# Two-input decode attention on one core: B's x loaded in 8-byte chunks behind the first K tile

## The chip, the cores and the metric

The kernel runs on one core of one Trainium2 chip. The metric is device microseconds (us) from start to end. An execution under the profiler has its own time, and a span (first to last instruction) that is a little shorter.

A core has a matrix engine (PE), a vector engine (DVE), an activation engine (ACT), a general engine (POOL) and a sync engine (SP). They run their own instruction streams and meet at semaphores. SP issues nearly all transfers here. A transfer is cut into packets that go to up to 16 DMA engines; each engine works through its own list in order. In this text such a list is called a ring: 16 rings, one per DMA engine. Behind the packets of a transfer each ring that took part writes the transfer's semaphore.

## The reference

Two independent attention blocks, A and B, each decode one token; their outputs are concatenated. Both have 32 heads of width 128, 8192 cached positions, and a model width of 512, all in bf16:

```
q      = (x @ wq)                  # x 1 x 512, wq 512 x 4096: 32 heads x 128
scores = q . K^T / sqrt(128)       # K per block 32 x 8192 x 128: 64 MB
p      = softmax(scores)
o      = p . V                     # V per block 32 x 8192 x 128: 64 MB
y      = o @ wo                    # wo 4096 x 512: 4 MB
out    = concat(y_A, y_B)          # 1 x 1 x 1024
```

Each K and V element is used once, so nearly all traffic is K and V: 4 x 64 MB, beside 4 MB for each of the four weight matrices and 1 KB for each x.

## The kernel before, in words

**Steps.** The work goes in 16 steps n = 0..15: 8 of A (n = 0..7), then 8 of B. A step takes four heads. Its K is one tile of 8 MB, 128 partitions x 256 positions x 128, 32 partitions to a head. `kn` holds two such tiles (slots n % 2), `vn` one V tile of the same size. In a step DVE multiplies the K tile by q in four chunks of 128 x 8192 (line 342, `plan_mul`). PE adds up the products by 16 matmuls with an identity per chunk (line 351, `plan_red`), and DVE reduces the result to scores (line 362, `plan_sr`). Then come the maximum (lines 368 to 391), the exponentials on ACT (line 399), and one step later the 256 matmuls with V (line 420, `plan_pv`). The last step is followed by the output projection (lines 478 and 505) and the output transfers.

**Loads.** All loads are issued by SP through `dma` (line 246) in the order in which the plan puts them. K of step n + 2 waits until step n has been summed (`red_done`), V of step n until the matmuls with the V before are done (`pv_done`), V of step 0 until all of q is made (`q_done[1]`). At the start SP issues five transfers without a wait: wq of A (4 MB, into the first half of `vn`), x of A, x of B (1 KB each), K of step 0 (8 MB), wq of B (4 MB, into the second half of `vn`). K of step 1 comes next. It goes to slot 1 of `kn`, and since the two x lie in partition 0 of that slot (`xrow`, with `KX = 1`), it waits for `x_ready`.

**x and q.** x arrives as one row in one partition. For each block four matmuls with a row of ones (line 302) spread it over the partitions, and ACT copies the result into `xb` (line 306). Before the change both blocks do this at the start, A through the PSUM tile `misc`, B through `qyp`; `x_ready` is the copy for B, the later one. `plan_q(a, j)` then makes q of four steps at a time: 16 matmuls with wq (line 320) into `qyp`, and an ACT copy into `qbc` (line 328). `qbc` has 16 slots of 128 elements per partition, 8 for A and 8 for B (`QA = 8`). q of A is made at the start. q of B is made inside step 0: on PE behind the third `plan_red`, ahead of the fourth.

**Order.** The order on each engine is written out by hand. PE runs steps 1 to 15 and the matmuls with V in a loop, and a final part comes after it. Names that the steps below touch: `load_k`, `load_x`, `load_wq`, `load_v`, `plan_x`, `plan_q`, `plan_red`, `plan_pv`, and the semaphores `s_x`, `s_w`, `s_k`, `s_v`.

Of the kernel before, what the change touches and what calls it, by code (L numbers as in the profile page):

```python
# [11 lines left out]
P = 128  # L12
# [11 lines left out]
class _Plan:  # L24
# [15 lines left out]
    def op(self, eng, fn, ctr=None, needs=(), inc=1):  # L40

        for m in needs:
            self.wait(eng, m)
        self.prog[eng].append((fn, ctr, inc))
        if ctr is None:
            return None
        ctr.n += inc
        return ctr, ctr.n
# [81 lines left out]
def bass_concat_heads__mha_block_cached__gqa_block_cached__decode_kernel(  # L130
# [13 lines left out]
    xs = [A_x, B_x]  # L144
# [4 lines left out]
    NA = 2  # L149
    H, Sk, Dh = ks[0].shape[1:]  # L150
    D = xs[0].shape[2]
    NOUT = wos[0].shape[1]
    assert Dh == P and H == 32 and D == 512 and NOUT == 512
    C = D // P
# [6 lines left out]
    QA = H // G  # L161
    NM = NA * QA
    NK = 2
    CT = 64
    NCH = T // CT
# [9 lines left out]
    with ExitStack() as st:  # L175
        ec = st.enter_context

        def sb(name, shape, dt):
            return ec(nc.sbuf_tensor(name, shape, dt))

        kn = sb("kn", [P, NK, T, Dh], BF16)
        vn = sb("vn", [P, T, Dh], BF16)

        def flat(ap):
            return ap.rearrange("p t d -> p (t d)")
# [5 lines left out]
        KX, KW = 1, (NM - 2) % NK  # L191
        wo_sb = [flat(kn[:, KW])[:, a * W:(a + 1) * W].rearrange("p (j n) -> p j n", n=NOUT)
                 for a in range(NA)]
        xrow = flat(kn[0:1, KX])[:, 0:NA * D].rearrange("p (a d) -> p a d", a=NA)
        xb = sb("xb", [P, NA, C, P], BF16)
        qbc = sb("qbc", [P, NM, Dh], BF16)
        pt = sb("pt", [P, T, G], BF16)
        s_sb = sb("s_sb", [P, T], F32)
        ones_bf = sb("ones_bf", [P, P], BF16)
# [19 lines left out]
        def ps(name, shape):  # L219
            return ec(nc.psum_tensor(name, shape, F32))  # L220
# [5 lines left out]
        misc = ps("misc", [P, 512])  # L226
        qyp = ps("qyp", [P, 512])
# [3 lines left out]
        op, wait = pl.op, pl.wait  # L231

        def ctr(name):
            return _Ctr(nc, st, name)

        s_x = ctr("s_x")
        s_w = [ctr("s_w%d" % a) for a in range(NA)]
        s_wo = [[ctr("s_wo%d%d" % (a, i)) for i in range(len(WOG[a]))] for a in range(NA)]
        s_k = [ctr("s_k%d" % i) for i in range(NK)]
# [2 lines left out]
        c_pool, c_dve, c_act, c_pe = ctr("c_pool"), ctr("c_dve"), ctr("c_act"), ctr("c_pe")  # L242
        c_mul, c_red, c_sr, c_pv = ctr("c_mul"), ctr("c_red"), ctr("c_sr"), ctr("c_pv")

        def dma(eng, dst, src, c, needs=()):
            return op(eng, lambda e: e.dma_start(dst, src), c, needs, inc=16)


        def const(fn, needs=()):
            return op("POOL", fn, c_pool, needs)  # L250

        i_onesb = const(lambda e: e.memset(ones_bf[:], 1.0))
# [15 lines left out]
        k_in, v_in, wq_in, wo_in = {}, {}, {}, {}  # L268
        red_done, pv_done, q_done, wo_done = {}, {}, {}, {}

        def quad(c, n):
            a, i = divmod(n, QA)
            return c[a][0, G * i:G * (i + 1)].rearrange("h (p t) d -> (h p) (t d)", p=HP)

        def load_k(n):
            k_in[n] = dma("SP", flat(kn[:, n % NK]), quad(ks, n), s_k[n % NK],
                          [x_ready if n == KX else red_done.get((n - NK, NCH - 1))])

        def load_v(n, cuts=(0, T)):
            dst, src = flat(vn[:]), quad(vs, n)  # L280
# [4 lines left out]
        def load_wq(a):  # L285
            wq_in[a] = dma("SP", wq_buf[a], wqs[a].rearrange("(p c) n -> p (c n)", p=P), s_w[a])

        def load_wo(a, g):
            h0, n = WOG[a][g]
            src = wos[a][h0 * Dh:(h0 + n) * Dh, :].rearrange("(p j) n -> p (j n)", p=P)  # L290
            wo_in[a, g] = dma("SP", wo_sb[a][:, h0:h0 + n, :].rearrange("p j n -> p (j n)"), src,
                              s_wo[a][g], [red_done[NM - 2, NCH - 1]])


        load_wq(0)
        x_in = [dma("SP", xrow[0:1, a, :], xs[a][0], s_x) for a in range(NA)][-1]

        for a in range(NA):
            def xmm(e, a=a):
                r = None  # L300
                for c in range(C):
                    r = e.matmul((misc if a == 0 else qyp)[:, c * P:(c + 1) * P],  # L302
                                 xrow[0:1, a, c:D:C], ones_bf[0:1, :], start=True, stop=True)
                return r
            m = op("PE", xmm, c_pe, [x_in, i_onesb])
            x_ready = op("ACT", lambda e, a=a: e.copy(
                xb[:, a].rearrange("p c m -> p (c m)"), (misc if a == 0 else qyp)[:]), c_act, [m])
        misc_free, qy_free = [x_ready], [x_ready]

        qbc_ready = {}  # L310

        def plan_q(a, j):

            def mm(e):
                r = None
                for hh in range(G):
                    for c in range(C):
                        w = wq_sb[a][:, c, 4 * G * j * Dh:4 * G * (j + 1) * Dh].rearrange(
                            "p (i h d) -> p i h d", h=G, d=Dh)[:, :, hh, :]
                        r = e.matmul(  # L320
                            qyp[hh * HP:(hh + 1) * HP, :].rearrange("p (i d) -> p i d", d=Dh),
                            xb[:, a, c, hh * HP:(hh + 1) * HP], w,
                            start=(c == 0), stop=(c == C - 1))
                return r
            m = op("PE", mm, c_pe, [x_ready, wq_in[a], qy_free[0]])
            q_done[a] = m
            n0 = a * QA + 4 * j
            qy_free[0] = op("ACT", lambda e: e.copy(  # L328
                qbc[:, n0:n0 + 4, :].rearrange("p i d -> p (i d)"), qyp[:]), c_act, [m])
            for n in range(n0, n0 + 4):  # L330
                qbc_ready[n] = qy_free[0]
# [8 lines left out]
        def plan_mul(n, c):  # L340
            k = kn[:, n % NK, c * CT:(c + 1) * CT, :]
            mul_done[n, c] = op("DVE", lambda e: e.tensor_tensor(  # L342
                k, k, qbc[:, nth(n), :].broadcast_to([P, CT, Dh]), ALU.mult),
                c_mul, [k_in[n], qbc_ready[n]])

        def plan_red(n, c):

            def mm(e, i0):
                r = None
                for i in range(Dh // DW):  # L350
                    r = e.matmul(  # L351
                        rps[:, c % 2, :].rearrange("p (t d) -> p t d", d=DW), ident[:],
                        kn[:, i0, c * CT:(c + 1) * CT, i * DW:(i + 1) * DW],
                        start=(i == 0), stop=(i == Dh // DW - 1))
                return r
            by_slot = (n % NK, [lambda e, i=i: mm(e, i) for i in range(NK)])
            red_done[n, c] = op("PE", by_slot, c_red, [
                i_ident, mul_done[n, c],
                sr_done[n, c - 2] if c > 1 else sr_done.get((n - 1, c + NCH - 2))])

        def plan_sr(n, c):
            sr_done[n, c] = op("DVE", lambda e: e.tensor_reduce(  # L362
                s_sb[:, c * CT:(c + 1) * CT],
                rps[:, c % 2, :].rearrange("p (t d) -> p t d", d=DW), AX.X, ALU.add),
                c_sr, [red_done[n, c], p_done.get(n - 1)])
# [62 lines left out]
        def plan_o(n):  # L428
            o_done[n] = op("DVE", lambda e: e.tensor_tensor(  # L429
                oD[:].rearrange("p a h -> p (a h)")[:, nth(n, G)], acc[:, 0:G],  # L430
                rinv[:, nth(n), :].rearrange("p o g -> p (o g)"), ALU.mult),
                c_dve, [pv_done[n], r_done[n]])
# [93 lines left out]
        cuts = {n: [] for n in range(L0, L1 + 1)}  # L526
        dcuts = []

        load_k(0)
        load_wq(1)  # L530
        ahead = len(pl.prog["SP"])
        plan_sel()
# [2 lines left out]
        for n in range(NM):  # L535
            if n >= L0:
                cuts[n].append(len(pl.prog["PE"]))
                dcuts.append(len(pl.prog["DVE"]))
            if n + 1 < NM:
                load_k(n + 1)  # L540
            else:
                load_wo(0, 0)
                for g in range(BEFORE):
                    load_wo(1, g)
            plan_mul(n, 0)
            plan_red(n, 0)
            plan_mul(n, 1)
            plan_red(n, 1)
            plan_sr(n, 0)
            plan_mul(n, 2)  # L550
            plan_red(n, 2)
            plan_sr(n, 1)
            plan_mul(n, 3)
            plan_sr(n, 2)
            if n == 0:
                for j in range(QA // 4):
                    plan_q(1, j)
            else:
                cuts[n].append(len(pl.prog["PE"]))
                plan_sum(n - 1)  # L560
                for t0, t1 in zip(VLAST, VLAST[1:]):
                    plan_pv(n - 1, t0, t1)
                cuts[n].append(len(pl.prog["PE"]))
                plan_o(n - 1)
            plan_red(n, 3)
            plan_sr(n, 3)
            plan_max(n)
            plan_gmax(n)
            plan_exp(n)
            load_v(n, VLAST if n == NM - 1 else (0, T))  # L570
# [112 lines left out]
```

## Time and profile before

| what | value |
|---|---|
| median of 3 runs | 667.17 us (666.86 to 667.19) |
| the profiled execution | 666.95 us |
| its span | 665.7 us |
| mean granted PE clock | 0.773 |
| busy share of the span: PE, DVE, ACT | 66%, 51%, 9% |
| moved | 285.33 MB, mean 429 GB/s |
| transfer packets | 6076, of them 690 under 512 bytes |

The profile's page cuts the span into 40 equal slices; a digit is the busy share of a slice in tenths. The windows view gives the same for chosen stretches. A row of the timeline is: start in us, duration in us, engine, line, operation, output tile <- input tile, sizes, count, and in brackets how long the engine had been idle before and what ended that. `SPq` rows are SP's issues of transfers; their duration is the time to issue, not to land. A row of waits is: engine, line, what was waited for, total us, times, longest us. A row of transfer issues ends with the median time from issue to landing. Line numbers are those of the kernel before.

### The profile page before, as it was taken

Reading aid. Unit: us, or ns where it says so; the run is one execution under the profiler, and the core shown is the slowest. Engines: PE = TensorE matmul, PEld = TensorE weight load, DVE = VectorE, ACT = ScalarE, POOL = GpSimd, SP = SyncE. Lnnn points to the kernel's source line nnn. Section 1 sums busy time; section 2 is a strip of 40 time slices with the busy share of each in tenths; the row PEclk is TensorE's granted clock in tenths of the full one; section 3 lists DMA queues with packets and bytes.
Section 4 is the critical chain, followed back from the end, with each engine's and each line's share of the span. In section 5 each row is a group of like instructions: output and inputs, shape, how many; then the busy total and the mean of one; then the engine's idle time right before and its main releaser. Section 6 shows DMA issues by size and latency. Waiting matters only on the chain. (4 is left out here: it accounts for less than half of the span.)

```text
span 665.7 us, 12460 instructions
## 1 busy us (share of the span) xinstructions
PE 440.0 (66%) x5649; PEld 253.2 (38%) x5649; DVE 340.4 (51%) x216; ACT 62.4 (9%) x151; POOL 3.0 (0%) x16
## 2 busy tenths in 40 slices
PE   1165776938388593838759483875948387694875
PEld 0022342616135261613526161442626144262655
DVE  1085908466390736638183563808356381835510
ACT  1002002020200102020110202010020201002020
POOL 1000000000000000000000000000000000000000
PEclk9999857768786676878767687966768787776875
DMA  9999999999999999999999999999999999999997
GB/s 378 435 447 438 438 432 417 425 437 441 425 437 441 441 425 422 433 441 433 429 441 437 437 421 425 441 437 425 441 437 441 421 425 437 441 425 437 414 439 303
DMA packets 6076, 285.33 MB, mean 429 GB/s; under 512 B 690, under 2 KB 948, under 8 KB 1204
## 3 DMA queue, kind: packets, MB, share of 16 engines
q1 hardware_dynamic: 6056, 285.22, 99.3%
q8 instruction: 6, 0.10, 0.1%
q14 instruction: 2, 0.02, 0.0%
q10 hardware_dynamic: 12, 0.00, 0.0%
HBM read 285.21 MB, written 0.00 MB: 428 GB/s over the span
## 5 line engine op out<-in xcount | busy, mean ns | idle before, releaser
L351 PE MATMUL rps<-kn,ident 128*128 128x512 bf16 x1024 | 291.2, 452 | 168.2 <-DVE kn L342 168.2
L342 DVE TENSOR_TENSOR kn<-kn,qbc 128x8192 bf16<-128x8192 bf16 x64 | 281.5, 4419 | 97.3 <-DMA kn<-in_A_k_cache_dram 57.6
L351 PEld LDWEIGHTS rps<-kn,ident 128*128 128x128 bf16 x1024 | 111.7, 113 | 334.8 <-issue 258.8
L420 PE MATMUL acc<-pt,vn 128*128 128x4 bf16 x4096 | 109.3, 165 | 9.8 <-DMA vn<-in_B_v_cache_dram 4.4
L420 PEld LDWEIGHTS acc<-pt,vn 128*128 128x128 bf16 x4096 | 108.6, 100 | 10.6 <-DMA vn<-in_B_v_cache_dram 4.8
L362 DVE TENSOR_REDUCE s_sb<-rps 128x64 f32<-128x512 f32 x64 | 44.0, 688 | 108.6 <-PE rps L351 108.6
L399 ACT ACTIVATE pt<-s_sb,negb 32x256 bf16<-32x256 f32 x64 | 54.9, 857 | 1.9
L391 ACT ACTIVATE negb<-bmp 128x1 f32<-128x1 f32 x16 | 2.7, 171 | 527.1 <-PE bmp L387 527.1
L429 DVE TENSOR_TENSOR oD<-acc,rinv 128x4 f32 (+1 forms) x16 | 2.6, 162 | 96.1 <-PE acc L420 84.9
L387 PE MATMUL bmp<-gm,hrow 1*128 1x1 f32 x128 | 17.6, 254 | 6.0 <-DVE gm L377 6.0
L387 PEld LDWEIGHTS bmp<-gm,hrow 1*128 1x128 f32 x128 | 16.2, 195 | 10.7 <-DVE gm L377 10.0
L374 PE MATMUL mtp<-ident_f,m 128*1 128x128 f32 x32 | 6.1, 270 | 19.8 <-DVE m L368 19.8
L399 ACT ACTIVATION_READ_ACCUMULATOR pt<-s_sb,negb 32x1 f32 x64 | 15.9, 248 | 0.0
L374 PEld LDWEIGHTS mtp<-ident_f,m 128*1 128x1 f32 x32 | 1.4, 80 | 27.7 <-DVE m L368 27.7
L302 PE MATMUL misc<-ones_bf,kn 1*128 1x128 bf16 x4 | 0.6, 302 | 13.1 <-DMA kn<-in_B_x_dram 13.1
L377 DVE TENSOR_REDUCE gm<-mtp 1x4 f32<-1x128 f32 x16 | 4.5, 279 | 7.5 <-PE mtp L374 7.5
L404 PEld LDWEIGHTS misc<-rsum,ones_f 128*128 128x128 f32 x32 | 6.2, 197 | 3.6 <-issue 1.4
L320 PE MATMUL qyp<-vn,xb 128*32 128x512 bf16 x64 | 6.0, 504 | 2.2 <-ACT qbc L328 1.5
L368 DVE TENSOR_REDUCE m<-s_sb 128x1 f32<-128x256 f32 x16 | 6.7, 420 | 0.5
L478 PE MATMUL qyp<-o,kn 128*128 128x1 bf16 x192 | 5.5, 165 | 1.7 <-issue 1.4
L478 PEld LDWEIGHTS qyp<-o,kn 128*128 128x128 bf16 x192 | 5.4, 103 | 1.9 <-issue 1.5
L328 ACT CAST qbc<-qyp 128x512 bf16<-128x512 f32 x4 | 2.3, 586 | 38.7 <-PE qyp L320 38.7
(39 smaller groups left out, 30.9 us busy)
## 6 DMA issues: line engine op xcount, KB each, us to landing
vn<-in_B_v_cache_dram SPq DMA_DIRECT2D x1, 6144.0 KB, 22.6
vn<-in_A_wq_dram SPq DMA_DIRECT2D x1, 4096.0 KB, 12.4
vn<-in_B_wq_dram SPq DMA_DIRECT2D x1, 4096.0 KB, 39.9
kn<-in_A_wo_dram SPq DMA_DIRECT2D x1, 4096.0 KB, 36.0
kn<-in_B_wo_dram SPq DMA_DIRECT2D x1, 2048.0 KB, 40.5
vn<-in_B_v_cache_dram SPq DMA_DIRECT2D x1, 2048.0 KB, 27.0
kn<-in_B_wo_dram SPq DMA_DIRECT2D x1, 1024.0 KB, 29.0
kn<-in_B_wo_dram SPq DMA_DIRECT2D x1, 512.0 KB, 29.8
```

The costliest lines, as they stand in the source:

```text
L320: r = e.matmul(qyp[hh * HP:(hh + 1) * HP, :].rearrange("p (i d) -> p i d", d=Dh), xb[:, a, c, hh * HP:(hh + 1) * HP], w, start=(c == 0), s ...
L342: mul_done[n, c] = op("DVE", lambda e: e.tensor_tensor(k, k, qbc[:, nth(n), :].broadcast_to([P, CT, Dh]), ALU.mult), c_mul, [k_in[n], qbc_ ...
L351: r = e.matmul(rps[:, c % 2, :].rearrange("p (t d) -> p t d", d=DW), ident[:], kn[:, i0, c * CT:(c + 1) * CT, i * DW:(i + 1) * DW], start= ...
L362: sr_done[n, c] = op("DVE", lambda e: e.tensor_reduce(s_sb[:, c * CT:(c + 1) * CT], rps[:, c % 2, :].rearrange("p (t d) -> p t d", d=DW), ...
L368: m_done[n] = op("DVE", lambda e: e.tensor_reduce(m1[:], s_sb[:], AX.X, ALU.max), c_dve, [sr_done[n, NCH - 1]])
L374: m = op("PE", lambda e: e.matmul(mtp[0:1, 0:P], m1[:], ident_f[:], start=True, stop=True), c_pe, [m_done[n], i_identf, gm_done.get(n - 1)])
L377: gm_done[n] = op("DVE", lambda e: e.tensor_reduce(gm[:], mtp[0:1, 0:P].rearrange("o (h p) -> o h p", h=G), AX.X, ALU.max), c_dve, [m, nb_ ...
L387: r = e.matmul(bmp[:, 0:1], hrow[0:1, h, :], gm[0:1, h:h + 1], start=(h == 0), stop=(h == G - 1))
L399: p_done[n] = op("ACT", lambda e, h=h, q=q: e.activation(pt[q, :, h], s_sb[q, :], AF.Exp, bias=negb[q, n:n + 1], scale=scale, accum_out=rs ...
L404: m = op("PE", lambda e: e.matmul(misc[:, 0:G], ones_f[:], rsum[:], start=True, stop=True), c_pe, [p_done[n], misc_free[0]])
L420: r = e.matmul(acc[:, 0:G], vn[:, t, :], pt[:, t, :], start=(t == 0), stop=(t == T - 1))
L478: r = e.matmul(qyp[:, i:i + 1], wo_sb[a][:, j, i * P:(i + 1) * P], o2[:, a, j:j + 1], start=(j == 0 and i == 0), stop=(j == HT[a] - 1 and ...
```

## The change

x of A is loaded alone, where both were. x of B gets a place of its own, and no longer in the slot of K: partition 0 of the part of `qbc` that later holds q of B, as 128 chunks of 4 elements (8 bytes) at every eighth element. It is loaded behind K of step 0 and ahead of wq of B, by 16 transfers of 15, 14, ... 1 and then 8 chunks, all on one semaphore `s_x1`. Its four matmuls and its copy are moved from the start to step 0, right ahead of q of B. K of step 1 and q of A wait for the copy of A's x alone. Both blocks go through `qyp`.

```
-        xrow = flat(kn[0:1, KX])[:, 0:NA * D].rearrange("p (a d) -> p a d", a=NA)
+        XCUTS = tuple(range(15, 0, -1)) + (8,)
+        assert sum(XCUTS) == P
...
+        xrow = [flat(kn[0:1, KX])[:, 0:D].rearrange("p (m c) -> p m c", c=C),
+                flat(qbc[0:1, QA:NM]).rearrange("p (m e) -> p m e", m=P)[:, :, 0:C]]
...
-        s_x = ctr("s_x")
+        s_x = [ctr("s_x%d" % a) for a in range(NA)]
...
-                          [x_ready if n == KX else red_done.get((n - NK, NCH - 1))])
+                          [x_ready[0] if n == KX else red_done.get((n - NK, NCH - 1))])
...
         load_wq(0)
-        x_in = [dma("SP", xrow[0:1, a, :], xs[a][0], s_x) for a in range(NA)][-1]
-
-        for a in range(NA):
-            def xmm(e, a=a):
+        def load_x(a, cuts):
+            src = xs[a][0].rearrange("o (m c) -> o m c", c=C)
+            m = 0
+            for n in cuts:
+                x_in[a] = dma("SP", xrow[a][:, m:m + n, :], src[:, m:m + n, :], s_x[a])
+                m += n
+
+        def plan_x(a):
+            def xmm(e):
                 r = None
                 for c in range(C):
-                    r = e.matmul((misc if a == 0 else qyp)[:, c * P:(c + 1) * P],
-                                 xrow[0:1, a, c:D:C], ones_bf[0:1, :], start=True, stop=True)
+                    r = e.matmul(qyp[:, c * P:(c + 1) * P], xrow[a][:, :, c], ones_bf[0:1, :],
+                                 start=True, stop=True)
                 return r
-            m = op("PE", xmm, c_pe, [x_in, i_onesb])
-            x_ready = op("ACT", lambda e, a=a: e.copy(
-                xb[:, a].rearrange("p c m -> p (c m)"), (misc if a == 0 else qyp)[:]), c_act, [m])
-        misc_free, qy_free = [x_ready], [x_ready]
+            m = op("PE", xmm, c_pe, [x_in[a], i_onesb, qy_free[0]])
+            x_ready[a] = qy_free[0] = op("ACT", lambda e: e.copy(
+                xb[:, a].rearrange("p c m -> p (c m)"), qyp[:]), c_act, [m])
+
+        x_in, x_ready = {}, {}
+        misc_free, qy_free = [None], [None]
+        load_x(0, (P,))
+        plan_x(0)
...
-            m = op("PE", mm, c_pe, [x_ready, wq_in[a], qy_free[0]])
+            m = op("PE", mm, c_pe, [x_ready[a], wq_in[a], qy_free[0]])
...
         load_k(0)
+        load_x(1, XCUTS)
         load_wq(1)
...
             if n == 0:
+                plan_x(1)
                 for j in range(QA // 4):
                     plan_q(1, j)
```

## The prediction

> **What bounds the kernel now.** I read the page first, its share of the transfer engines above all.
>
> ```profile
> PE 440.0 (66%) x5649; PEld 253.2 (38%) x5649; DVE 340.4 (51%) x216; ACT 62.4 (9%) x151; POOL 3.0 (0%) x16
> DMA  9999999999999999999999999999999999999997
> DMA packets 6076, 285.33 MB, mean 429 GB/s; under 512 B 690, under 2 KB 948, under 8 KB 1204
> q1 hardware_dynamic: 6056, 285.22, 99.3%
> q8 instruction: 6, 0.10, 0.1%
> q14 instruction: 2, 0.02, 0.0%
> ```
>
> No compute engine is busy for more than two thirds of the span; SP's queue (q1) keeps the 16 rings busy for 99.3% of it. The bytes stay as they are, so an edit can move the time in three ways only: by letting the rings run dry, by adding to what a ring has to work off, or at the two ends. The windows show how far the middle is from dry, and the ends:
>
> ```profile
> 0.00:5.00 5.00, 0.00 (x0) 0.00 (x0) 2.29 (x10) 1.28 (x1) 3.01 (x16) 1.00 0.66 216
> 300.00:400.00 100.00, 74.83 (x974) 42.87 (x975) 56.69 (x32) 7.21 (x18) 0.00 (x0) 0.77 1.01 436
> 655.00:660.00 5.00, 5.00 (x193) 5.00 (x191) 0.00 (x0) 0.00 (x0) 0.00 (x0) 0.50 0.96 398
> 660.00:665.70 5.70, 2.69 (x86) 2.03 (x83) 0.91 (x4) 0.00 (x0) 0.00 (x0) 0.50 0.32 120
> ```
>
> The last three columns are granted clock, DMA share and GB/s: full in the middle, short only in the first and the last microseconds. The timeline of the end shows who waits for whom:
>
> ```profile
> 653.54 7.02 PE L420 MATMUL acc<-pt,vn 128*128 128x4 bf16 x256 [3.43 <-DMA vn<-in_B_v_cache_dram]
> 661.48 1.02 PE L505 MATMUL yrow<-kn,o 128*1 128x128 bf16 x32 [0.92 <-PEq L604]
> 663.14 0.47 PE L505 MATMUL yrow<-kn,oD 128*1 128x128 bf16 x8
> 663.67 0.29 DVE L516 CAST out_q<-yrow 128x128 bf16<-128x128 f32 x1 [0.85 <-PE yrow L505]
> 663.99 0.58 SPq L246 DMA_DIRECT2D out_dram<-out_q  x2
> ```
>
> PE stood for 3.43 us until the first part of the last V had landed, at 653.54, and from there it is 12 us of PE work to the end. A landing counts when the last of 16 rings is through, so the end hangs on the slowest ring. No view splits the rings. I followed them through the trace's packet records (each packet of a ring starts where the one before ends); this table is worked out from them. Rings are numbered from the one that took both x packets, in the order of their first packets; the four-row output transfer, whose packets also start there, took numbers 0 to 3.
>
> ```
> ring                          0      1      2      3      4      5      6      7
> last V load done, us        655.86 656.81 657.29 655.77 657.80 657.57 657.42 657.33
> code block fetched at, us     -    256.8   87.7    -    651.4   97.1   89.7   82.4
> ring                          8      9     10     11     12     13     14     15
> last V load done, us        656.20 655.83 656.05 656.23 656.02 656.22 657.31 657.38
> code block fetched at, us     -      -      -      -      -      -    643.6   53.4
> ```
>
> The eight packets of the instruction queues (q8, q14 above) each fell on a ring of its own and set it back, the 16 KB ones by about 1.5 us; the rings without one finish last V near 656. Ring 4 is the slowest at 657.80, the mean is 656.69. So a ring in 0 or 8 to 13 can be delayed by over 1.5 us for nothing, and ring 4 by nothing.
>
> **The change, part by part.** The rows of the start:
>
> ```profile
> 1.62 0.22 SPq L246 DMA_DIRECT2D kn<-in_B_x_dram  x1
> 1.88 0.36 SPq L246 DMA_DIRECT2D kn<-in_A_k_cache_dram  x1
> 2.28 0.51 SPq L246 DMA_DIRECT2D vn<-in_B_wq_dram  x1
> 13.10 0.61 PE L302 MATMUL misc<-ones_bf,kn 1*128 1x128 bf16 x4 [13.10 <-DMA kn<-in_B_x_dram]
> 13.74 0.58 ACT L306 CAST xb<-misc 128x512 bf16<-128x512 f32 x1 [11.67 <-PE misc L302]
> 14.22 0.59 ACT L306 CAST xb<-qyp 128x512 bf16<-128x512 f32 x1
> 14.84 0.33 SPq L246 DMA_DIRECT2D kn<-in_A_k_cache_dram  x1
> 32.53 8.76 DVE L342 TENSOR_TENSOR kn<-kn,qbc 128x8192 bf16<-128x8192 bf16 x2 [28.75 <-DMA kn<-in_A_k_cache_dram]
> ```
>
> 1. x of B leaves the start. A 1 KB packet with its semaphore goes from ring 0 (48 ns in the packet records), and ring 0 has 1.9 us in hand: nothing. A's copy is ready at 14.32 and not 14.81, so K of step 1 is issued and q of A made 0.49 us earlier. Both are early already: K's predecessor in the rings lands at 32.5, and the first multiply waits for that landing, 28.75 us idle. Nothing. That A goes through `qyp` and not `misc` costs nothing either, since q of A, which writes `qyp`, waited for the later copy before.
>
> 2. Sixteen issues on SP ahead of wq of B. A 1 KB issue took 0.22 us here, so 16 take 3.5, and at the 0.51 of the row behind it 8.2. wq of B is issued at 5.5 to 10.2 and not 2.28, K of step 1 still at about 14.3.
>
> ```profile
> vn<-in_B_wq_dram SPq DMA_DIRECT2D x1, 4096.0 KB, 39.9
> vn<-in_A_v_cache_dram SPq DMA_DIRECT2D x8, 31.5
> ```
>
> wq of B takes 39.9 us from issue to landing, of which its 4 MB need about 10 at the mean rate. It stands in the rings for some 30 us behind K, and 8 us of that can go: nothing. Were that cover gone, each further microsecond on SP would be one of dry rings.
>
> 3. The 128 packets. I take a transfer of n chunks as n packets on rings 0 to n-1, as the output's four rows made four. Then ring r gets one packet and one semaphore write from each transfer larger than r: 16 on ring 0, 12 on ring 4, 11 on ring 5, 1 on ring 14, none on ring 15. What a pair costs the ring no row shows. The nearest records: a 4-byte semaphore write 9 ns, 256 bytes 15, 1,024 bytes 46, each overlapping the next by 3 or 4. By these a pair of 8 and 4 bytes takes 12 ns, and the slow ring 4 loses 12 x 12 = 0.15 us. The dear end is from the landings: ring 0's two x semaphores were written 48 ns apart and took effect at 12.86 and 13.05, 187 ns apart. If every ordered write holds the ring for that long, ring 4 loses 12 x 187 = 2.2 us. I take 12 ns, since the 64 KB packet behind those two writes started at once and took 2,418 ns like all others. The other rings do not pass ring 4 at either price: ring 1 would need 330 ns a pair, ring 0 over 500.
>
> The page "DMA: Bandwidth & Descriptors" of the Trainium skill says under "Queues, rings and completion order" that a semaphore increment lands only after every earlier write of that DMA engine. The 187 ns agree with a wait of that kind for the increment; whether data behind it waits too no run here shows. By this rule alone, taken as holding the ring, the sum would be 2.2 us; by the packet records it is 0.15. The same page puts line rate at 512 bytes and more, with a read-modify-write below; our 4-byte records of 9 ns do not show such a price, and no 8-byte write into a tile is in this trace's queue q1.
>
> 4. x of B inside step 0. Its four matmuls and copy now stand ahead of q of B on PE: 13.10 to 14.32 in the rows above, 1.22 us, with the hand-over 1.3.
>
> ```profile
> 52.33 1.08 PE L320 MATMUL qyp<-vn,xb 128*32 128x512 bf16 x16
> 55.31 0.33 SPq L246 DMA_DIRECT2D vn<-in_A_v_cache_dram  x1
> 58.82 0.33 SPq L246 DMA_DIRECT2D kn<-in_A_k_cache_dram  x1
> 60.44 0.28 DVE L377 TENSOR_REDUCE gm<-mtp 1x4 f32<-1x128 f32 x1 [0.47 <-PE mtp L374]
> 62.87 8.76 DVE L342 TENSOR_TENSOR kn<-kn,qbc 128x8192 bf16<-128x8192 bf16 x2 [2.15 <-DMA kn<-in_A_k_cache_dram]
> 93.46 0.33 SPq L246 DMA_DIRECT2D vn<-in_A_v_cache_dram  x1
> ```
>
> What queues behind: the fourth sum on PE, DVE's last reduction and maximum, and on SP V of step 0 and K of step 2. V's issue goes from 55.31 to 56.6. K of step 1 holds the rings until about 60.3 (its landing ends DVE's wait at 62.87), and from SP's first issue at 0.80 to the first packet went 1.0 us, so V's packets stand ready at 57.6: 2.7 us of cover. K of step 2 goes to 60.1 and is due when V is through, some 19 us later. DVE is free for step 1 at 62.0 and not 60.72; it waits until 62.87 anyway. Nothing, with 0.9 us to spare; if that went, step 1 would start late by the rest, and its next issue, at 93.46 with V's median 31.5 us from issue to landing against 19 of transfer, has several microseconds in the ring.
>
> The sum: 0 + 0 + 0.15 + 0 on the profiled execution's 666.95 gives 667.10. The median of the runs shown is 667.17, 0.22 above it; on that basis 667.3.
>
> **The rivals.**
>
> *Slower: ordered writes hold the rings.* The dear end of part 3: 16 transfers, each closed by a semaphore write on each ring that took part, 187 ns apiece. Ring 4 then ends 2.2 us later, and the end with it: 669.4. It leaves the 0.2% band (1.33 us, about what a measurement of this kernel can tell from no change) from 111 ns a transfer on ring 4. For it: the two landings. Against it: the K packet right behind them lost nothing, but two are few, and a buffer could hide two and not twelve.
>
> *Faster: the code fetches meet the rings in another order.* Ring 4's fetch at 651.4 falls just ahead of the landing that PE waits for. PE's instruction stream is re-ordered ahead of the loop, and if a fetch goes to one of the idle rings, ring 5 sets the end: 657.57 for 657.80, 0.2 us less, 667.0. All rings even would be 656.69, 1.1 us less: 666.1. So even this does not reach 0.2%. Against it: PE has the same matmuls as before, and of the low rings, which get the packets, six of eight are late as it is.
>
> *Slower: the rings run dry at step 0.* If part 4 came to over 4 us and not 1.3, V of step 0 would be late. It takes a wait that I do not see, such as x of B not landed by 52: it is queued behind a K that lands at 32.5. Each microsecond beyond is one at the end; 3 us of it give 669.
>
> *The chunks do not spread.* If all 128 go on ring 0, that is 1.5 us at 12 ns on a ring with 1.9 us in hand: 667.2, no change.
>
> The section "Why a DMA increments its semaphore by 16 and not by 1" of the same Trainium skill page says that the chunks' count, up to 16, sets how many engines take part, from the lowest number up; that agrees with one x packet and four output packets here, and would make the spread that of part 3.
>
> **How the numbers follow.** The likeliest, cheap packets, 0.58, with pair prices up to 60 ns: 667.0 to 667.9, likeliest 667.3. Held rings, 0.27: 667.9 to 669.4, more if a small write into a tile costs beyond its semaphore. Dry rings or a longer step 0, 0.06: 668 to 670. Fetches met otherwise, 0.09: 666.1 to 667.0. The range is 666.7 to 669.5: it leaves out the lower half of the last case, and what lies above the dear end. Faster by over 0.2% takes more than even rings could give: 0.05. Slower by over 0.2% is most of the held rings and the dry ones: 0.31. Within: 0.64.
>
> **What would show it.** Packets of the page: about 6076 - 2 + 256 = 6330, and SP's 16 issues between 1.9 and 10 us. V of step 0 issued at about 56.6, step 1's first multiply still ended by K's landing at 62.9: part 4 right. That landing 1 to 2 us later, and PE's last wait for V ending at 655 or beyond: held rings. That wait ending within 0.3 us of 653.54: cheap packets. The prediction is wrong if a DMA digit in the first three slices drops, or if the landings of the end move by over 1.3 us.

## The result and the profile after

| | before | changed |
|---|---|---|
| median (22 runs each) | 666.95 us | 667.87 us (667.50 to 668.72) |
| ratio, 95% interval | | 1.0015 (1.0009 to 1.0021) |
| profiled execution / its span | 666.95 / 665.7 us | 668.72 / 667.4 us |

The change costs 0.92 us (the ratio's estimate is 0.15%): more than the noise of these runs, less than the prediction's band of 0.2%. The profiled execution of the changed kernel happens to be the slowest of its 22 runs, 0.85 us above their median; a second trace of the same kernel (experiment 8) is closer to it, and the difference between the two is told there.

The page of the changed kernel, the lines that answer to those of before:

```profile
PE 446.6 (67%) x5649; PEld 255.1 (38%) x5649; DVE 340.4 (51%) x216; ACT 62.6 (9%) x151; POOL 3.0 (0%) x16
DMA packets 6330, 285.33 MB, mean 428 GB/s; under 512 B 945, under 2 KB 1202, under 8 KB 1458
q1 hardware_dynamic: 6310, 285.22, 99.2%
q8 instruction: 6, 0.10, 0.1%
q14 instruction: 2, 0.02, 0.0%
```

The packets are 6330, as counted in advance (128 chunks and 128 semaphore writes for one of each). The rings are as busy as before, the bytes the same. The timeline of SP at the start, and DVE's start of step 1:

```profile
2.00 11.61 SPq L249 DMA_DIRECT2D qbc<-in_B_x_dram  x16
13.65 0.44 SPq L249 DMA_DIRECT2D vn<-in_B_wq_dram  x1
14.19 0.38 SPq L249 DMA_DIRECT2D kn<-in_A_k_cache_dram  x1
55.92 0.33 SPq L249 DMA_DIRECT2D vn<-in_A_v_cache_dram  x1
60.53 0.33 SPq L249 DMA_DIRECT2D kn<-in_A_k_cache_dram  x1
98.37 0.33 SPq L249 DMA_DIRECT2D vn<-in_A_v_cache_dram  x1
...
62.15 0.28 DVE L389 TENSOR_REDUCE gm<-mtp 1x4 f32<-1x128 f32 x1 [0.47 <-PE mtp L386]
64.78 8.76 DVE L354 TENSOR_TENSOR kn<-kn,qbc 128x8192 bf16<-128x8192 bf16 x2 [2.35 <-DMA kn<-in_A_k_cache_dram]
```

Step 1 starts at 64.78 and not 62.87, and still DVE waits there for K's landing: the rings are 1.9 us late by then. Where it happened is read off wq of B, the transfer right behind the chunks. Its row in the list of transfer issues gives the time from issue to landing:

```profile
vn<-in_B_wq_dram SPq DMA_DIRECT2D x1, 4096.0 KB, 30.5
```

Issued at 13.65, landed at 44.2. Before, it was issued at 2.28 and landed at 42.2 (39.9 later). So the last ring lost 2.0 us between K of step 0 and the end of wq of B. The end of the kernel, in the timeline of the changed kernel:

```profile
655.23 7.01 PE L432 MATMUL acc<-pt,vn 128*128 128x4 bf16 x256 [1.75 <-DMA vn<-in_B_v_cache_dram]
663.21 1.02 PE L517 MATMUL yrow<-kn,o 128*1 128x128 bf16 x32 [0.96 <-PEq L618]
665.46 0.29 DVE L528 CAST out_q<-yrow 128x128 bf16<-128x128 f32 x1 [0.92 <-PE yrow L517]
```

PE's wait for the last V ends 1.69 us later, and all behind it follows 1.7 to 1.8 us later. The kernel still ends with its slowest ring.

**What the packet records show.** The records of single packets, which no view lists, show the chunks themselves: a chunk and its semaphore write are 12 ns of a ring, as costed. But the packets behind them are longer than the 1,213 ns that a 32 KB packet of wq of B takes otherwise: the first two on eight of the sixteen rings, by over 1 us together, and the first one on two rings more. The number of transfers that a ring took part in can be matched from the length of its row of small packets. The match is certain for the first and the last rings and the best fit between neighbours:

```
transfers that used the ring   16   15   14   13   12   11   10    9    7    6   5 to 0
extra time behind them, us   2.08 1.68 1.48 1.48 1.46 1.43 1.12 1.14 0.33 0.18    0
```

### The profile page after: what moved, and what is told of

Same layout as the page of the kernel before. It is cut to its first block, busy times and chain, and to the rows that moved or that the text cites. A ratio compares the mean times of both kernels' runs of the same rounds, so it can differ in the third digit from the quotient of the medians.

```text
span 667.4 us, 12476 instructions
## 1 busy us (share of the span) xinstructions
PE 446.6 (67%) x5649; PEld 255.1 (38%) x5649; DVE 340.4 (51%) x216; ACT 62.6 (9%) x151; POOL 3.0 (0%) x16
## 2 busy tenths in 40 slices
DMA packets 6330, 285.33 MB, mean 428 GB/s; under 512 B 945, under 2 KB 1202, under 8 KB 1458
## 3 DMA queue, kind: packets, MB, share of 16 engines
q1 hardware_dynamic: 6310, 285.22, 99.2%
## 5 line engine op out<-in xcount | busy, mean ns | idle before, releaser
L363 PE MATMUL rps<-kn,ident 128*128 128x512 bf16 x1024 | 296.8, 459 | 164.1 <-DVE kn L354 164.1
L363 PEld LDWEIGHTS rps<-kn,ident 128*128 128x128 bf16 x1024 | 113.1, 114 | 335.3 <-issue 262.1
L441 DVE TENSOR_TENSOR oD<-acc,rinv 128x4 f32 (+1 forms) x16 | 2.6, 163 | 95.8 <-PE acc L432 86.2
L416 PE MATMUL misc<-rsum,ones_f 128*128 128x4 f32 x32 | 4.8, 220 | 1.3 <-issue 1.3
```

The lines of the kernel that those rows point to most:

```text
L363: r = e.matmul(rps[:, c % 2, :].rearrange("p (t d) -> p t d", d=DW), ident[:], kn[:, i0, c * CT:(c + 1) * CT, i * DW:(i + 1) * DW], start= ...
L416: m = op("PE", lambda e: e.matmul(misc[:, 0:G], ones_f[:], rsum[:], start=True, stop=True), c_pe, [p_done[n], misc_free[0]])
```

## The experiments

Three theories stood at the start. Theory 1: each transfer ends on each of its rings with a semaphore write that waits until all writes before it are done, some 0.2 us apiece, and holds the ring. Theory 2: the small packets hold it. Theory 3: the moves cost, and not the packets: x of B in step 0, SP's sixteen issues, code fetched at other moments. All edits are to the changed kernel, and all runs are timed against the kernel before on the same chip. "Wait ends" is where PE's last wait for V ends in the profiled execution (653.54 before).

| | median, us | kernel before | ratio (95%) | wq of B landed | wait ends |
|---|---|---|---|---|---|
| 1 one packet | 666.89 | 666.95 | 1.0000 (0.9991 to 1.0009) | 42.2 | 653.30 |
| 2 one transfer of 128 | 667.09 | 666.95 | 1.0004 (0.9995 to 1.0013) | 42.4 | 653.54 |
| 3 sixteen on ring 0 | 667.26 | 666.95 | 1.0004 (0.9995 to 1.0013) | 44.0 | 654.01 |
| 4 sixteen on 8 rings | 669.02 | 666.95 | 1.0030 (1.0019 to 1.0041) | 44.5 | 655.75 |
| 5 eight on 16 rings | 667.60 | 666.95 | 1.0010 (1.0001 to 1.0019) | 43.1 | 654.07 |
| 6 2-byte packets | 671.84 | 666.95 | 1.0075 (1.0061 to 1.0088) | 47.0 | 657.75 |
| 7 two groups | 667.34 | 666.95 | 1.0005 (0.9995 to 1.0014) | 43.0 | 654.03 |
| 8 changed again | 668.01 | 666.95 | 1.0016 (1.0007 to 1.0025) | 43.9 | 654.64 |
| 9 512 packets of 8 bytes | 668.57 | 666.78 | 1.0027 (1.0017 to 1.0038) | 44.2 | 655.04 |
| 10 4-byte packets | 668.06 | 666.78 | 1.0021 (1.0011 to 1.0031) | 44.0 | 654.58 |
| 11 sixteen of 1 KB on ring 0 | 667.38 | 666.78 | 1.0008 (0.9998 to 1.0017) | 44.2 | 653.97 |

**1. One packet.** The move without the chunks.

```
-        XCUTS = tuple(range(15, 0, -1)) + (8,)
+        XCUTS = (P,)
...
-                flat(qbc[0:1, QA:NM]).rearrange("p (m e) -> p m e", m=P)[:, :, 0:C]]
+                flat(qbc[0:1, QA:NM])[:, 0:D].rearrange("p (m c) -> p m c", c=C)]
```

> x of B goes to the same place in the queue and in the order, but into 512 adjacent elements of q's tile, by one transfer of one packet (1 KB, ring 0). Theory 1 (each transfer's ordered semaphore write holds its ring for some 0.2 us): one such write, on a ring with 1.9 us in hand; as the kernel before, 666.9 to 667.1. Theory 2 (the small packets themselves cost): the same, 667.0. Theory 3 (what was moved costs: x of B inside step 0, later V of step 0, other meeting of code fetches): as slow as the changed kernel, 667.9.

666.89, the same as before: what was moved costs nothing. Theory 3 falls, and with it every rival about step 0. V of step 1 is issued 2.5 us later than before here too, and nothing comes of it:

```profile
95.95 0.33 SPq L249 DMA_DIRECT2D vn<-in_A_v_cache_dram  x1
653.30 7.01 PE L432 MATMUL acc<-pt,vn 128*128 128x4 bf16 x256 [1.34 <-DMA vn<-in_B_v_cache_dram]
```

**2. One transfer of 128 chunks.** The packets without the sixteen semaphore writes.

```
-        XCUTS = tuple(range(15, 0, -1)) + (8,)
+        XCUTS = (P,)
```

> The same 128 chunks of 8 bytes in one transfer: 8 packets and one semaphore write on each of the 16 rings, one issue on SP. Theory 1: one ordered write per ring, no hold, 0.1 us of packets; 667.0 to 667.1. Theory 2 (8-byte packets hold a ring, 0.1 us each beyond a few): every ring loses as a ring with 8 packets did in the changed kernel, 0.3 to 1.1 us, so 667.3 to 668.0. Theory 3: 667.9.

```profile
2.63 0.60 SPq L249 DMA_DIRECT2D vn<-in_B_wq_dram  x1
vn<-in_B_wq_dram SPq DMA_DIRECT2D x1, 4096.0 KB, 39.8
```

wq of B lands at 42.4. The first packet behind the chunks is longer by 0.04 to 0.11 us on 15 rings and by 0.33 on one, and the run is 0.14 us above before, with an interval that includes no change. So eight 8-byte packets in a row cost a ring next to nothing.

**3. Sixteen transfers, all on ring 0.** As experiment 1, with `XCUTS = (8,) * 16`: each transfer is 64 adjacent bytes, one packet.

> Sixteen transfers of 64 adjacent bytes each: one packet each, all on ring 0, so 16 semaphore writes on ring 0 and none on the others; SP issues 16 as in the changed kernel. Theory 1: ring 0 is held by some 2.1 us, of which 1.9 are its slack against the slowest ring; 667.0 to 667.3, and the rows of wq of B's landing show one ring late. Theory 2: sixteen packets on ring 0 alone, the same. If SP's sixteen issues or x of B's late landing cost by themselves: 667.9 as the changed kernel.

```profile
2.02 4.72 SPq L249 DMA_DIRECT2D qbc<-in_B_x_dram  x16
6.78 0.35 SPq L249 DMA_DIRECT2D vn<-in_B_wq_dram  x1
vn<-in_B_wq_dram SPq DMA_DIRECT2D x1, 4096.0 KB, 37.2
654.01 7.05 PE L432 MATMUL acc<-pt,vn 128*128 128x4 bf16 x256 [2.08 <-DMA vn<-in_B_v_cache_dram]
```

wq of B lands at 44.0, as late as in the changed kernel, because one ring is late: the two packets behind the small ones were 1.35 and 0.50 us longer. The sixteen semaphore writes took effect over 2.70 us, 0.18 us apart. And yet the end moves by only 0.3 to 0.5 us (the interval includes no change), since ring 0 ended last V 1.9 us ahead of the slowest before. Ring 0 ends it at 658.20 in this trace, against 657.80 of the slowest before: both the hold and the slack are as the theory has them.

**4. Sixteen transfers of 8 chunks.** `XCUTS = (8,) * 16` with the chunks where they were.

> Sixteen transfers of 8 chunks: 16 packets and 16 semaphore writes on each of rings 0 to 7, none on 8 to 15. Theory 1: rings 0 to 7 are held alike, by what ring 0 was in the changed kernel, 2.1 us; rings 4 and 5, the slowest, end 0.6 to 0.7 us later than in the changed kernel: 668.4 to 668.7. Theory 2: the same by the packets, 668.5. Theory 3 (what was moved, not the writes): 667.9, as the changed kernel.

```profile
2.00 10.68 SPq L249 DMA_DIRECT2D qbc<-in_B_x_dram  x16
12.72 0.45 SPq L249 DMA_DIRECT2D vn<-in_B_wq_dram  x1
vn<-in_B_wq_dram SPq DMA_DIRECT2D x1, 4096.0 KB, 31.8
655.75 7.02 PE L432 MATMUL acc<-pt,vn 128*128 128x4 bf16 x256 [0.84 <-DMA vn<-in_B_v_cache_dram]
```

Exactly eight rings have long packets behind the chunks, 1.8 to 2.4 us each, and the median is 2.07 us higher; the execution of this trace took 669.24, 2.29 more than before's 666.95. That is more than the 668.4 to 668.7 expected; which ring makes the difference is told under experiment 8.

**5. Eight transfers of 16 chunks.** `XCUTS = (16,) * 8`: each ring has 8 packets, as in experiment 2, but 8 semaphore writes for one.

> The 128 chunks in 8 transfers of 16: 8 packets and 8 semaphore writes on each of the 16 rings, against 8 packets and one write in the one-transfer run, which came to 667.09. Theory 1 (the back-to-back ordered writes hold the ring): every ring is held by between 0.33 and 1.14 us, what rings with 7 and 9 transfers lost in the changed kernel; the first packets of wq of B are longer on all 16; 667.4 to 668.1. Theory 2 (the packets): the same as one transfer, 667.1.

```profile
7.05 0.59 SPq L249 DMA_DIRECT2D vn<-in_B_wq_dram  x1
vn<-in_B_wq_dram SPq DMA_DIRECT2D x1, 4096.0 KB, 36.0
654.07 7.01 PE L432 MATMUL acc<-pt,vn 128*128 128x4 bf16 x256 [1.24 <-DMA vn<-in_B_v_cache_dram]
```

All sixteen rings are held by some 0.45 to 1.0 us, and the kernel is 0.65 us slower, where the same packets in one transfer came to 0.14 (its slowest run, 667.41, is below the fastest here, 667.47). The difference is seven more transfers a ring, each with its semaphore write: theory 1.

**6. Packets of 2 bytes.** x of B in one transfer to every second element: 512 packets, 32 and one semaphore write on each ring. (All transfers carry the flag that allows such pieces.)

```
...
+                flat(qbc[0:1, QA:NM]).rearrange("p (m c e) -> p m c e", c=C, e=2)[:, :, :, 0]]
```

> x of B in one transfer of 512 packets of 2 bytes: 32 packets and one semaphore write on each ring, four times the packets of the one-transfer run. Theory 1: 32 packets of some 6 ns and one write: 0.2 to 0.3 us over the kernel before, 667.1 to 667.3. Theory 2 (small packets hold a ring by 10 ns and more each, as the 0.05 to 0.11 us of the one-transfer run could be read): 0.4 us of hold on top, 667.5 or more.

```profile
2.63 0.81 SPq L249 DMA_DIRECT2D vn<-in_B_wq_dram  x1
vn<-in_B_wq_dram SPq DMA_DIRECT2D x1, 4096.0 KB, 44.4
657.75 7.01 PE L432 MATMUL acc<-pt,vn 128*128 128x4 bf16 x256 [3.14 <-DMA vn<-in_B_v_cache_dram]
```

A miss for theory 1 alone: every ring loses over 4 us, wq of B lands 4.8 us later than before, and the kernel is 4.9 us slower. Small packets do hold a ring, too. Whether by their number or their size, experiments 9 and 10 were to tell.

**7. Two groups.** The transfers of 15, 13, ... 1 chunks stay ahead of wq of B; those of 14, 12, ... 2 and 8 go behind it.

```
...
-        load_x(1, XCUTS)
+        load_x(1, XCUTS[0::2])
         load_wq(1)
+        load_x(1, XCUTS[1::2], sum(XCUTS[0::2]))
```

> The changed kernel's 16 transfers in two groups: those of 15, 13, ... 1 chunks ahead of wq of B, those of 14, 12, ... 2 and 8 behind it. Each ring has the same writes as in the changed kernel, but at most 8 in a row; ring 4 has 6 and 6. Theory 1 with a reserve (up to five writes in a row cost nothing, as on rings 10 to 15 of the changed kernel): ring 4 loses 0.2 us twice with the packets' 0.15, 667.3 to 667.5. Theory 1 without one (each write costs alike wherever it stands): as the changed kernel, 667.9.

667.34. The same writes in two groups of at most eight on a ring cost 0.39 us, with an interval that includes no change, where the unsplit kernel cost 1.06 on the same chip (experiment 8); and no run of the one lies among those of the other (667.55 at most, 667.79 at least). So a ring has a reserve of a few transfers that it takes without loss, and much of it is there again 10 us later. It is not sharply five: the second group, ahead of K of step 1, left long packets on eight rings, 0.27 to 0.87 us, and by the count rings with five transfers in it are among them.

**8. The changed kernel again.** No edit.

> The changed kernel once more, for a trace nearer to its median, on the chip of these runs: 667.9. By theory 1 the same eight rings are held at wq of B by 1.1 to 2.1 us. If the half microsecond by which its profiled execution stood above its median came from the rings running dry near 99 us, V of step 1 is issued earlier in this trace than 98.37 or the slowest ring loses nothing there.

```profile
64.40 8.76 DVE L354 TENSOR_TENSOR kn<-kn,qbc 128x8192 bf16<-128x8192 bf16 x2 [2.00 <-DMA kn<-in_A_k_cache_dram]
96.17 0.33 SPq L249 DMA_DIRECT2D vn<-in_A_v_cache_dram  x1
654.64 7.01 PE L432 MATMUL acc<-pt,vn 128*128 128x4 bf16 x256 [0.73 <-DMA vn<-in_B_v_cache_dram]
```

Eight rings are held by 0.9 to 2.0 us here. The wait ends 1.10 us later than before, and this execution took 668.12, 1.17 more than the 666.95 of before's: the rings account for all of it. In the other trace it was 0.6 us more. There the latest ring was 0.4 us later by the landing of K of step 1, and V of step 1 was issued at 98.37 for 96.17 here. That is behind a stall of PE in the first trace, 4.87 us where the trace of experiment 8 has 2.84:

```profile
97.06 1.28 PE L432 MATMUL acc<-pt,vn 128*128 128x4 bf16 x42 [4.87 <-issue]
```

No wait in the profile ends it; PE goes on 2.4 us after the packet of a 16 KB code block starts, at 94.62 here and at 92.49 in experiment 8, so I take it that PE stands for its code. The first rings were through with K of step 2 at about 99.2, ran dry for up to a microsecond, and the next transfer started cold: from the landing of K to that of V the last ring took 19.58 us and not 19.35. So this execution is slower by 0.2 us on top. (In experiment 4's trace V of step 1 is issued at 98.22 and some rings run dry as well; its last ring took 19.34 us, so there it cost nothing.)

*Which ring sets the end.* This trace, and that of experiment 4, show which rings the fetched code blocks fall on. Those of 52.6 and 86.2 us and the two of 8 KB fall on held rings, and those of 92.5, 99.4, 647.5 and 653.5 outside the eight (in experiment 4, 53.5, 85.1 and the first of 8 KB on held rings, 94.6, 99.2 and 648.3 outside). If the blocks go to the same rings in the kernel before, the ring that was last there, with the fetch at 651.4, is not among the eight that the chunks hold. The ring of the fetch near 53 us is. Before, it finished last V at 657.38. In this trace it was held by 1.30 us, and with 0.13 for its 11 pairs (by the match above) it should end at 658.81; it ended at 658.96, the latest of all, 1.16 behind the 657.80 of before's slowest. In experiment 4 that ring was held by 2.24 us and 16 pairs add 0.19: 659.81 worked out, 659.90 in the trace. One ring is later still there, by the same match the one of the block at 85.1, held by 2.25: it ends at 660.08, 2.28 behind, and the execution of that trace was 2.29 slower.

**9. 512 packets of 8 bytes.** Experiment 1 with one more transfer that nobody uses, 4 KB of K, and K of step 1 waiting for it.

```
...
+        extra = [dma("SP", flat(kn[0:1, KX])[:, 1024:5120].rearrange("p (n e) -> p n e", e=8)[:, :, 0:4],
+                     ks[1][0, 0:1, 0:16, :].rearrange("o t d -> o (t d)").rearrange("o (n c) -> o n c", c=4),
+                     ctr("s_extra"))]
```

> The one-packet kernel (666.89) with one more transfer behind x of B that nobody uses: 512 packets of 8 bytes out of K of B into slot 1 of kn, 32 packets and one semaphore write on each ring, as the two-byte run had (671.84), but of 8 bytes each. K of step 1 waits for its landing. If it is the number of small packets that held the rings in the two-byte run: 671 to 672. If it is the size of 2 bytes, and an 8-byte packet costs no more than its 6 ns and a little (theory 1): 32 x 6 ns and 0.1, so 667.1 to 667.4.

```profile
2.95 0.66 SPq L249 DMA_DIRECT2D vn<-in_B_wq_dram  x1
vn<-in_B_wq_dram SPq DMA_DIRECT2D x1, 4096.0 KB, 41.2
655.04 7.01 PE L432 MATMUL acc<-pt,vn 128*128 128x4 bf16 x256 [1.46 <-DMA vn<-in_B_v_cache_dram]
```

Between the two expectations. 32 packets of 8 bytes in a row hold the ring by 0.8 to 1.6 us, on most by 1.5; with 0.2 for the packets that gives the 1.79 measured. Against the 0.08 or so of 8 packets (experiment 2) that is 0.06 us for each further packet, a third of what a semaphore write costs. The 2-byte packets, as many, cost 4.9 us: there the size counts as well.

**10. Packets of 4 bytes.** x of B in one transfer of 256, 16 packets and one semaphore write on each ring; the four matmuls read it through a matching access pattern.

```
...
+                flat(qbc[0:1, QA:NM]).rearrange("p (m e) -> p m e", m=2 * P)[:, :, 0:2]]
```

> x of B as 256 packets of 4 bytes in one transfer: 16 packets and one semaphore write on each ring. If the number of small packets in a row holds a ring (8 of them: 667.09, 32 of 2 bytes: 671.84), some 16 x 0.15 us less a reserve of about 1 us: 668 to 669. If only 2-byte packets do: 667.1 to 667.3.

1.28 us over before. Eleven rings show a long packet behind the small ones, by 0.2 to 1.1 us, with no pattern that I can name, and the runs spread from 667.43 to 669.24. Sixteen packets of 4 bytes cost more than the 0.7 us that lies on the line from experiment 2 (8 of 8 bytes, 0.14) to experiment 9 (32, 1.79); how the price depends on the size stays open.

**11. Sixteen transfers of 1 KB on ring 0.** As experiment 9, with sixteen contiguous transfers of 1 KB for the one.

```
...
+        for i in range(16):
+            extra = [dma("SP", flat(kn[0:1, KX])[:, 1024 + i * D:1024 + (i + 1) * D],
+                         ks[1][0, 0:1, 4 * i:4 * i + 4, :].rearrange("o t d -> o (t d)"), ex)]
```

> The one-packet kernel with sixteen more transfers that nobody uses, of 1 KB each, one packet and one semaphore write apiece, all on ring 0; the ring-0 run had 64-byte packets there and lost 1.84 us in the first two packets of wq of B. Theory 1 (the ordered writes hold the ring, whatever the packets' size): 16 x 0.2 us less the 16 x 46 ns that the packets take and the reserve: the next packet on ring 0 is still 0.8 to 1.5 us long; 667.3 to 668.2, since ring 0 loses over 1.9 us with the packets' own 0.8. Theory 2 (only packets under 512 bytes hold): no long packet behind them, ring 0 loses 0.8 us of its slack, 666.9 to 667.0.

667.38, 0.60 over before; the interval includes no change, but the fastest run here (667.17) is above the slowest of before (667.07). The two packets behind the sixteen are 0.96 and 0.23 us longer, where 64-byte packets left 1.35 and 0.50, and the semaphore writes took effect 0.18 us apart again. The last two of the 1 KB packets themselves took 158 and 185 ns where the others took 46: by then the ring moves at the pace of the writes. So transfers with their writes hold a ring though none of their data packets is under 1 KB, which rules out small packets as the whole cause. No run has a transfer without its semaphore write; that it is the write, and not something else at a transfer's end, is read from the 0.18 us between the landings.

## Why the prediction was right in its number and wrong in its cause

The time, 667.87, lies in the range of 666.7 to 669.5, and the move stays within 0.2% as forecast. The forecast's own time, 667.3, was 0.57 us low, and the case behind it, cheap packets, is not what happened. The rival "ordered writes hold the rings" is, at less than its price. That the time came out near the forecast is in part luck: two errors worked against each other (part 3).

*The signs named in advance.* K of step 1 landed 1.9 us later and PE's wait ended at 655.23 in the first trace: held rings, by the prediction's own words. Its sign of being wrong, landings of the end that move by over 1.3 us, is there in that trace too (1.69 us), and not in the second (1.10).

*What bounds the kernel.* Right: the slowest ring sets the landing of the last V, and a delay of that ring comes out at the end one for one (experiments 4 and 8).

*Parts 1 and 4, the moves.* Right in the sum: experiment 1 does them without the chunks and takes the same time as before. V of step 0 was issued at 55.92, 0.6 us later and not 1.3; K of step 2 at 60.53 for a forecast 60.1. The cover of several microseconds for V of step 1 was not so: it was issued 2.5 us later in experiment 1 and 4.9 later in the first trace of the changed kernel, where the fast rings did run dry. It cost 0.2 us there and nothing in experiment 4, the other trace in which they did.

*Part 2, SP's issues.* Right that they are covered, low in their price: 11.61 us for sixteen, 0.73 each, where a contiguous one takes 0.3 (4.72 for sixteen in experiment 3). K of step 1 was issued at 14.19 only because the sixteen just fitted ahead of it.

*Part 3, the packets.* This is the step that failed, twice. The pair was put at 12 ns, 0.15 us in the sum, because the K packet behind two semaphore writes lost nothing. The 12 ns are right as time on the ring. But the writes behind each other take effect 0.18 us apart, as the landings of the two x (187 ns) had shown. In this kernel a ring takes about five such transfers without loss, so two could not show it; with 9 to 16 it is held by 1.1 to 2.1 us. How much of that is the small packets' own is not separated: sixteen 8-byte packets behind one write were not run, but sixteen writes with 64-byte packets held ring 0 by 1.85 (experiment 3). The other error was the ring. I numbered the rings by the order of their first packets and made the slowest one number 4, with 12 of the transfers. By experiments 4 and 8 it is none of the eight held rings, if the code blocks fall on the same rings as before. A ring that had 0.4 us in hand, held by about 1.3 us, took its place. The two errors partly cancel: ring 4 held by 1.46 us and with its packets' 0.14 would have made 1.6 us; the ring that did become the last makes 1.16. (A slip beside it: ring 0, 1.94 us ahead with four pairs more, would pass ring 4 at 485 ns a pair, not at over 500. Nothing hangs on it.)

*The rule of the Trainium skill.* The page "DMA: Bandwidth & Descriptors" of the Trainium skill, section "Queues, rings and completion order", has the semaphore write wait for every earlier write of its engine. The traces agree with such a wait: 0.18 us from one such write to the next. That data behind the writes waits too is not on the page; the runs show it, with more than about five in a row. The same page of the Trainium skill, section "Specifications", has a transfer under 512 bytes as a read-modify-write; experiments 6, 9 and 10, whose loss one semaphore write a ring cannot explain, agree in direction, but no run shows that this is the reason.

*The chances.* "Slower by over 0.2%" had 0.31 and did not come. The held rings, with a chance of 0.27, were put at 667.9 to 669.4 and gave 667.87, which is also the upper end of cheap packets: the time alone could not tell the two apart, the landings did.

## What to carry to other kernels

Where one transfer follows another on all rings without a gap, the number of transfers behind each other has a price of its own: about five small ones in a row were free here (fewer in experiment 7), and each further one held its ring by some 0.2 us (0.16 to 0.29 in the changed kernel's first trace). Bring a small operand in one transfer of one packet (no change here), and if it has to be many transfers, spread them between large ones. A kernel bound by its rings is bound by the slowest of them, so a small loss on all is worse than a large one on a ring that is early: 1.85 us on ring 0 cost 0.3, and 0.45 to 1.0 us on every ring cost 0.65.

## What the runs showed of the hardware that was not expected

- Semaphore writes of successive transfers on one ring take effect 0.18 us apart (2.70 us for sixteen with 64-byte packets, 2.72 with 1 KB packets), while the packet records show them 12 ns apart, or about 50 with 1 KB packets.
- 32 packets in a row on every ring cost 1.8 us at 8 bytes and 4.9 at 2 bytes, with one semaphore write in both.
- A fetched 16 KB block of code delays the one ring that it falls on by 1.5 us, and in a kernel bound by the rings the delay stays until the end (before, the rings without a block finish last V near 656, those with a 16 KB one at 657.3 to 657.8).
- SP's issue of a transfer of 8-byte chunks takes 0.6 to 0.73 us, of a contiguous one 0.3.
